# Two attentions in one kernel: maxima in the last projection product, the start, and one copy

## The chip, the cores and the metric

The kernel runs on one core of a Trainium2 chip. The metric is the device time of one execution in microseconds (us); the time of a kernel is the median of its runs.

## The reference

Two attention layers of the same shape (2,048 positions, 576 features, 32 heads of 18) stand side by side in the output. Layer A is local and dilated: a query sees eight keys, two positions apart. Layer B is a full softmax attention.

```python
qkv = (x @ wqkv).reshape(B, S, 3, H, Dh)            # S = 2048, D = 576, H = 32, Dh = 18
# A: keys at pos - 2*j, j = 0..7
logits = jnp.einsum("bhsd,bhswd->bhsw", q, kg) * scale ; mask
o = jnp.einsum("bhsw,bhswd->bhsd", softmax(logits), vg)
# B:
scores = jnp.einsum("bhqd,bhkd->bhqk", q, k) * scale
o = jnp.einsum("bhqk,bhkd->bhqd", softmax(scores), v)
# both: o.reshape(B, S, D) @ wo, and concatenate([a, b], axis=-1)
```

Everything is in single precision. The kernel keeps it with products of operands that are split into a high and a low part.

## The kernel before, in words

The order of the instructions on each engine is written by hand: what the program emits first stands first. Work for later is put in an agenda by step (`later`, `plan`), and `slot` and `due` emit what is due.

The stages, by the clock of the profiled execution:

1. *0 to 44 us.* Inputs are loaded and split, first products of layer B (L595). Ahead of them stand warm products of zeros (L561), whose results nobody reads, and the load of the exponential's table on ACT with its first use (L404).
2. *44 to 81 us.* The values of layer B (L317).
3. *81 to 402 us.* The other projections, of both layers. `stream` takes the products four at a time, in pairs of halves of the rows, and sets maxima in between (`most(j)` says how many pairs of maxima are given by the end of product j). A projection product of A leaves through `leave_a`, by a copy on ACT (L747) into `ohi`, and goes to DRAM.
4. *402 to about 1,448 us.* The attention steps of B: 512 steps, which are 32 blocks (eight groups of four heads, four blocks of 512 queries) of 16 key tiles. A step has four scores on PE (L285), four exponentials on ACT (L293), and the four weighings by the values into `po` (L800). In between PE makes maxima of later blocks (L161), VectorE reduces them (L169), and POOL computes the local attention A.
5. *To the end.* The output sums: beside the steps (`beside`, L1246), in pieces between them (L1278), and at the end. Each finished row block `y` is added on VectorE (L1285) and stored by SP (`out<-y`, L1315).

The softmax of B subtracts a row maximum ahead of the exponential. It enters the scores as two more rows of the operand `qs` (high and low part, `mh` and `mt`). A block needs 32 pairs of maxima, 1,024 pairs in all: of a pair, one matmul (L161) uses each half of the array's rows, and one reduction belongs to each. After a block's last reduction come `least` (L179), in the next step the transpose (L186), then the split on POOL (L104, L105), and then eight small DMAs on SP (`place`, L200) into `qs`. A block's first scores wait for these eight. Steps make one and a half pairs each (one whole pair, one in halves of 256 columns), and use up two; so the lead with which blocks are finished shrinks towards the end. `EARLY_PAIRS` pairs are made ahead of the first step.

There are seven PSUM banks in rotation: four for scores, three ("else") for maxima and products in the attention stage. SP is one queue, and issues in order: `qs<-mh` and `qs<-mt` are L200, `y<-wob` loads output weights (L954), `do<-n` stores a block's attention result (L835), `ks<-do` and `qs<-do` load such results back (L1171).

The lines that set the counts of maxima before:

```python
few = 7 * (NT - 4) // 4
folded_ = [args[0] == "folded" for args, _, _ in work_list]
plain = [sum(not f for f in folded_[NT - 4 : j + 1]) for j in range(len(work_list))]
most = [few + 2 * sum(folded_[:j + 1]) + (EARLY_PAIRS - few - 2 * sum(folded_)) * p // plain[-1]
        for j, p in enumerate(plain)]
```

Of the kernel before, what the change touches and what calls it, by code (L numbers as in the profile page):

```python
# [7 lines left out]
F32 = mybir.dt.float32  # L8
F32R = mybir.dt.float32r
BF16 = mybir.dt.bfloat16  # L10
AF = mybir.ActivationFunctionType
# [12 lines left out]
NT = S // 128  # L24
NB = S // 512
# [10 lines left out]
PIECES = 2 * 4 * NB  # L36


EARLY = 2
EARLY_PAIRS = EARLY * NB * PIECES + 2  # L40
AHEAD = 7

AT = [10, 67] + [13 + 55 * j for j in range(2, S // AB)]
# [18 lines left out]
def two_attentions(ctx: ExitStack, tc, xa, wa, woa, xb, wb, wob, out):  # L62
# [5 lines left out]
    nc = tc.nc  # L68
# [13 lines left out]
    def bank(kind=None):  # L82
        r = rings[kind or ring]
        r.append(r.pop(0))
        return p_bank.tile([128, 512], F32, name=f"bank{r[-1]}")
# [13 lines left out]
    ones = const.tile([2, 128], F32, name="ones")  # L99
    nc.gpsimd.memset(ones, 1.0)  # L100
    warm = const.tile([2, 8], F32, name="warm")
# [249 lines left out]
    def stream(products, most, last):  # L351

        where, ends = {}, {}  # L360
        for j in range(len(products)):
            first = j - j % 4
            turn = [((0, 0), (1, 1)), ((0, 2), (1, 3)), ((0, 1), (1, 0)), ((0, 3), (1, 2))][j % 4]
            both = []
            for r, k in turn:
                args, view, _ = products[first + k]
                if j % 4 < 2:
                    where[k] = view(bank("scores"))
                else:
                    assert sum(given) - ends[k] > 3  # L370
                parts = folded(r, *args[1:]) if args[0] == "folded" else halves(r, *args)
                both.append([(where[k], *ab, j % 4 < 2 and i == 0, j % 4 > 1 and i == len(parts) - 1)
                             for i, ab in enumerate(parts)])
            n = most(j) - given[0]
            others = last if j == len(products) - 1 else ([], [])
            n += 2 if others[0] else 0
            total = n + len(both[0])
            for r in range(2):
                for i in range(n):
                    both[r].insert((4 * i + 1 + 2 * r) * total // (4 * n), None)  # L380
            for pair in zip(*both):
                for r, p in enumerate(pair):
                    if p is None:
                        (others[r].pop(0) if others[r] else maximum(r))()
                    else:
                        ps, a, b, start, stop = p
                        nc.tensor.matmul(ps, a, b, start=start, stop=stop)  # L387
            for k in sorted(k for _, k in turn):
                if j % 4 < 2:
                    ends[k] = sum(given)  # L390
                else:
                    products[first + k][2](where[k])
            slot()
            for _ in range(min(len(posts), 2)):
                posts.popleft()()
        do_all(posts)
# [4 lines left out]

    every = slice(0, 512)

    nc.scalar.activation(warm, ones[:, :8], AF.Exp)  # L404

    with (tc.tile_pool(name="x", bufs=1, side="right") as xp,
          tc.tile_pool(name="a0", bufs=1, side="right") as a0):
        raw_room = ExitStack()
        rp = raw_room.enter_context(tc.tile_pool(name="rows", bufs=1, side="right"))
# [29 lines left out]
        def weights(pool, src, cols, engine, wide=384, spare=False):  # L439

            whole = [[], [], None, None]
            n = sum(m for _, m in cols)

            def into(c, t):
                if c < 4:
                    hi, lo = (pool.tile([128, wide], F32R, name=nm, bufs=4) for nm in ("whi", "wlo"))
                    whole[0].append(hi)
                    whole[1].append(lo)
                else:
                    hi, lo = (pool.tile([128, wide], F32R, name=nm, bufs=1) for nm in ("whh", "wll"))  # L450
                    whole[2:] = hi, lo
                split(engine, hi[:, :n], lo[:, :n], t)

            apart = cols[1][0] - cols[0][0] if len(cols) > 1 else n
            return whole, *staged(src, cols, [(apart, len(cols)), (1, cols[0][1])], into, spare)
# [59 lines left out]
        def folds(c):  # L515
            return c == 13
# [13 lines left out]
        if True:  # L530
# [3 lines left out]
            def turn_cols(i):  # L534
                return [(third * i, third), (D + third * i, third)]
# [19 lines left out]
                        at += n  # L555


            zeros = rp.tile([128, 512], F32, name="raw", bufs=5)
            nc.vector.memset(zeros, 0.0)
            for _ in range(2):  # L560
                nc.tensor.matmul(bank(), zeros[:, :128], zeros, start=True, stop=True)  # L561
            w0, w_get, w_put = weights(proj[0], wb, turn_cols(0), nc.vector, spare=True)

            xs = [inputs(xb, b, nc.vector, spare=b != 2) for b in range(NB)]
            for c in range(5):
                one, other = (load, nc.scalar.dma_start) if c % 2 == 0 else (nc.scalar.dma_start, load)
                w_get(c, one)
                xs[0][1](c, other if c < 4 else load)
            for b in range(1, NB):
                for c in range(5):  # L570
                    xs[b][1](c)
# [76 lines left out]
            for t in range(NT):  # L648
                ps = bank()
# [87 lines left out]
            def leave_a(c, b, n, ps):  # L737
                o = xp.tile([128, 512], F32, name="ohi", bufs=4)
                at = slice(0, n)
                if folds(c):  # L740
                    at, other = (slice(64 * r, 64 * r + 64) for r in (b % 2, 1 - b % 2))
                    rest = ws[c][0][2].bitcast(F32)
                    nc.scalar.activation(rest[at], ps[other], AF.Copy)
                    nc.scalar.activation(o[at], ps[at], AF.Copy)
                    nc.gpsimd.tensor_add(o[at], o[at], rest[at])
                else:
                    nc.scalar.activation(o[at], ps[at], AF.Copy)  # L747
                load(da[128 * c : 128 * c + n, HALO + 512 * b : HALO + 512 * b + 512], o[at])


            order = [t for i in (0, 8) for j in range(4) for t in (i + j, i + j + 4)]
            for t in order[:4]:
                ps = bank()
# [5 lines left out]
            work_list = []  # L759
# [10 lines left out]
            order = [(c, b) for b0 in range(0, NB, 2) for c in range(2) for b in (b0, b0 + 1)]  # L770
            order += [(c, b) for c in sorted(range(2, 14), key=a_place) for b in range(NB)]
            for c, b in order:
                n = min(128, 3 * D - 128 * c)
                work_list.append((("folded", ws[c][0], xas[b][0]) if folds(c) else
                                  (b % 2, ws[c][0], xas[b][0], slice(0, n), every),
                                  lambda ps: ps, lambda ps, c=c, b=b, n=n: leave_a(c, b, n, ps)))
            es = [None] * 4
            few = 7 * (NT - 4) // 4
            folded_ = [args[0] == "folded" for args, _, _ in work_list]
            plain = [sum(not f for f in folded_[NT - 4 : j + 1]) for j in range(len(work_list))]  # L780
            most = [few + 2 * sum(folded_[:j + 1]) + (EARLY_PAIRS - few - 2 * sum(folded_)) * p // plain[-1]
                    for j, p in enumerate(plain)]
            stream(work_list, lambda j: 7 * (j + 1) // 4 if j < NT - 4 else most[j],
                   [[lambda r=r: es.__setitem__(r, score(0, 0, 0, r, "else")), lambda r=r: maximum(r)(),
                     lambda r=r: es.__setitem__(r + 2, score(0, 0, 0, r + 2, "else"))] for r in range(2)])
# [623 lines left out]
    while step < ALL:  # L1409
        n, kt = divmod(step, NT)  # L1410
        g, b = divmod(n, NB)
# [23 lines left out]
        ps = bank() if inside and whole else None  # L1435
# [67 lines left out]
```

## Time and profile before

| | |
|---|---|
| median of 3 runs | 1578.12 us (1577.4 to 1578.15) |
| profiled execution | 1577.92 us, span 1576.1 us |
| granted TensorE clock | 1.00 in all windows |
| PE busy | 1566.0 us (99%) |
| DVE busy | 1375.7 us (87%) |
| ACT busy | 1210.7 us (77%) |
| POOL busy | 975.9 us (62%) |

The span is the time from the first to the last instruction on the chip; 1.8 us of the measured time lie outside it. PEld is the load of weights into the array, which can lie beside a product. A bracket behind a row of the timeline says how long its engine had stood idle before it and what ended that ("issue" where the profile shows no releaser). A timeline row with xN holds N instructions of one form, and its duration runs from the first to the last of them.

### The profile page before, as it was taken

The page shows a single profiled execution, that of the slowest core. Times are in us where ns is not written, and L with a number is a line of the kernel's source. Part 1 is how long each engine was busy: PE and PEld are TensorE (multiplying, and loading weights), DVE is VectorE, ACT ScalarE, POOL GpSimd, SP SyncE. Part 2 cuts the span into 40 slices and gives each one's busy share as a digit, 9 for nine tenths or more (in the row PEclk, how much of TensorE's full clock was granted, in tenths as well). Part 3 has the DMA queues.
Part 4 walks back from the last instruction along what each step waited for, and adds up shares of the span by engine and source line. Part 5 has one row for each costly group of instructions (what it writes and reads, how often), then busy time and mean ns, then how long its engine had stood idle before and what let it go on. Part 6 is the DMA issues. An engine that isn't in the chain of part 4 may idle for free.

```text
span 1576.1 us, 34876 instructions
## 1 busy us (share of the span) xinstructions
PE 1566.0 (99%) x13236; PEld 967.7 (61%) x13236; DVE 1375.7 (87%) x2333; ACT 1210.7 (77%) x2415; POOL 975.9 (62%) x807
## 2 busy tenths in 40 slices
PE   9999999999999999999999999999999999999998
PEld 7999999999544445445445445445444444545686
DVE  5189999999999999999999999999999999998633
ACT  6324432122799999999999999999999999998554
POOL 2316752212256995995896896897797798782000
PEclk9999999999999999999999999999999999999999
DMA  8848954532312362254325324422721331154311
GB/s 259 230 142 217 268 167 125 145 107 74 68 50 57 81 140 83 55 126 101 74 82 130 86 90 112 117 79 53 150 81 50 91 101 53 50 164 136 138 57 69
DMA packets 188168, 175.65 MB, mean 111 GB/s; under 512 B 119432, under 2 KB 133512, under 8 KB 186272
## 3 DMA queue, kind: packets, MB, share of 16 engines
q1 hardware_dynamic: 182992, 161.73, 37.5%
q0 software_dynamic: 4032, 10.63, 3.3%
q8 instruction: 104, 1.70, 0.5%
q10 hardware_dynamic: 976, 1.07, 0.2%
q14 instruction: 64, 0.52, 0.1%
HBM read 98.77 MB, written 73.47 MB: 109 GB/s over the span
## 4 chain that ended last, share of the span: by engine, by line
PE 95%; DVE 3%; DMA 1%; ACT 0%; POOL 0%; issue 0%; SPq 0%; DVEq 0%; POOLq 0%; ACTq 0%
PE po L800 30%; PE bank L285 19%; PE bank L161 18%; PE bank L387 16%; PE bank L1381 4%; PE bank L1278 3%; DVE mx L169 2%; PE bank L595 2%; PE bank L317 2%; DMA dqk<-olo 1%; PE bank L1246 0%; DMA first<-xb 0%; ACT e L293 0%; PE bank L1210 0%; POOL olo L549 0%
## 5 line engine op out<-in xcount | busy, mean ns | idle before, releaser
L169 DVE TENSOR_REDUCE mx<-bank 128x2 f32<-128x512 f32 x2048 | 1276.8, 683 | 109.5 <-PE bank L161 82.2
L293 ACT ACTIVATE e<-bank 128x512 f32<-128x512 f32 x2048 | 1047.7, 604 | 81.5 <-PE bank L285 77.1
L161 PE MATMUL bank<-ks,qs 54*128 54x512 f32 (+1 forms) x2464 | 784.6, 380 | 2.4 <-DVE mx L169 0.5
L161 PEld LDWEIGHTS bank<-ks,qs 54*128 54x128 f32 x2464 | 402.8, 184 | 388.7 <-DVE mx L169 343.4
L285 PE MATMUL bank<-qs,ks 56*128 56x512 f32 x2048 | 591.6, 425 | 0.0
L800 PE MATMUL po<-e,v 128*19 128x512 f32 x4096 | 531.8, 598 | 0.4
L285 PEld LDWEIGHTS bank<-qs,ks 56*128 56x128 f32 x2048 | 308.6, 184 | 20.4 <-ACT e L293 14.5
L1021 POOL TENSOR_TENSOR pr<-aq,akv 128x1024 f32<-128x1024 f32 x72 | 158.5, 2203 | 15.5 <-DMA akv<-da 12.7
L1063 POOL TENSOR_TENSOR pr<-lg,akv 128x1024 f32<-128x1024 f32 x72 | 158.3, 2199 | 0.6
L800 PEld LDWEIGHTS po<-e,v 128*19 128x19 f32 x4096 | 73.5, 97 | 138.5 <-issue 133.2
L1025 POOL TENSOR_TENSOR pr<-pr 128x1024 f32<-128x1024 f32 x64 | 152.7, 2385 | 5.0
L747 ACT ACTIVATE ohi<-bank 128x512 f32<-128x512 f32 x52 | 28.2, 595 | 139.1 <-issue 111.7
L387 PE MATMUL bank<-xhi,ahi 64*128 64x512 f32 x448 | 113.2, 386 | 0.0
L387 PE MATMUL bank<-xlo,ahi 64*128 64x512 f32 x448 | 107.6, 387 | 0.0
L1381 PE MATMUL bank<-wohi,at 64*128 64x288 f32 x480 | 103.3, 304 | 0.0
L387 PE MATMUL bank<-xhi,alo 64*128 64x512 f32 x416 | 103.0, 387 | 0.0
L1064 POOL TENSOR_TENSOR pr<-pr 128x512 f32<-128x512 f32 x72 | 92.5, 1285 | 5.6
L1381 PEld LDWEIGHTS bank<-wohi,at 64*128 64x128 f32 x480 | 74.6, 184 | 27.5 <-ACT e L293 23.8
L549 POOL TENSOR_TENSOR olo<-olo,ohi 128x512 fp32r<-128x512 f32 x36 | 46.2, 1293 | 68.3 <-ACT ohi L548 60.7
L437 POOL TENSOR_TENSOR alo<-raw,ahi 128x512 fp32r<-128x512 f32 x13 | 16.9, 1296 | 113.6 <-ACT ahi L436 79.7
L104 POOL CAST mh<-mt 128x32 fp32r<-128x32 f32 x32 | 6.8, 212 | 110.6 <-DVE mt L186 85.5
L1381 PE MATMUL bank<-wolo,at 64*128 64x288 f32 x240 | 70.2, 293 | 0.0
(215 smaller groups left out, 1856.2 us busy)
## 6 DMA issues: line engine op xcount, KB each, us to landing
do<-n SPq DMA_DIRECT2D x30, 512.0 KB
da<-ohi SPq DMA_DIRECT2D x52, 256.0 KB
akv<-da SPq DMA_DIRECT2D x64, 175.5 KB
out<-y SPq DMA_DIRECT2D x31, 288.0 KB
qs<-dqk SPq DMA_DIRECT2D x30, 288.0 KB
ks<-dqk SPq DMA_DIRECT2D x30, 288.0 KB
at<-dao SPq DMA_DIRECT2D x60, 128.0 KB
rec<-drec SPq DMA_DIRECT2D x29, 256.0 KB
```

The lines of the kernel that those rows point to most:

```text
L161: return awaiting(nc.tensor.matmul(ps if part is None else ps[:, 256 * r : 256 * r + 256], qs[at, b, p, 128 * t : 128 * t + 128], ks[at, p ...
L169: nc.vector.tensor_reduce(at, ps.rearrange("q (s n) -> q s n", s=2), axis=AX.X, op=ALU.max)
L285: awaiting(nc.tensor.matmul(ps, ks[at, p, 128 * kt : 128 * kt + 128], qs[at, b, p], start=True, stop=True))
L293: nc.scalar.activation(e, ps, AF.Exp, scale=SCALE)
L387: nc.tensor.matmul(ps, a, b, start=start, stop=stop)
L800: nc.tensor.matmul(po[32 * i : 32 * i + 19], vs[g][:, kt, 19 * i : 19 * i + 19], es[i], start=kt == 0, stop=kt == NT - 1)
L1021: nc.gpsimd.tensor_mul(pr, ap(st["q"][:, 2 * c], (SUB, 2), (0, W), (1, SUB)), window(st["k"], c))
L1025: nc.gpsimd.tensor_add(st["pr"], st["pr"], pr)
L1063: nc.gpsimd.tensor_mul(at, ap(st["lg"], (0, 2), (SUB, W), (1, SUB)), window(st["v"], c))
L1064: nc.gpsimd.tensor_add(at[:, :, :4], at[:, :, :4], at[:, :, 4:])
L1278: nc.tensor.matmul(sums_[r], *both[r][i], start=i == 0, stop=last)
L1381: return nc.tensor.matmul(ps, a, b, start=r == k == 0, stop=r == 1 and k == len(both[1]) - 1)
```

## The change

Four edits. `EARLY_PAIRS` is 256 instead of 258, and the counts are by rule: two pairs in a folded product, three in another, and what is left, two, in the last. The first use of the exponential's table stands behind ACT's four first DMA issues. Nine warm products of 128 columns take the place of two of 512. The last product of A's projection is copied out of its bank by VectorE.

```diff
-EARLY_PAIRS = EARLY * NB * PIECES + 2
+EARLY_PAIRS = EARLY * NB * PIECES
...
-    nc.scalar.activation(warm, ones[:, :8], AF.Exp)
...
-            zeros = rp.tile([128, 512], F32, name="raw", bufs=5)
+            zeros = rp.tile([128, 512], F32, name="raw", bufs=5)[:, :128]
             nc.vector.memset(zeros, 0.0)
-            for _ in range(2):
-                nc.tensor.matmul(bank(), zeros[:, :128], zeros, start=True, stop=True)
+            for _ in range(9):
+                nc.tensor.matmul(bank()[:, :128], zeros, zeros, start=True, stop=True)
...
                 xs[0][1](c, other if c < 4 else load)
+            nc.scalar.activation(warm, ones[:, :8], AF.Exp)
...
+                elif (c, b) == order[-1]:
+                    nc.vector.tensor_copy(o[at], ps[at])
                 else:
                     nc.scalar.activation(o[at], ps[at], AF.Copy)
...
-            folded_ = [args[0] == "folded" for args, _, _ in work_list]
-            plain = [sum(not f for f in folded_[NT - 4 : j + 1]) for j in range(len(work_list))]
-            most = [few + 2 * sum(folded_[:j + 1]) + (EARLY_PAIRS - few - 2 * sum(folded_)) * p // plain[-1]
-                    for j, p in enumerate(plain)]
+            narrow = [args[0] == "folded" for args, _, _ in work_list]
+            each_takes = [0] * (NT - 4) + [2 if f else 3 for f in narrow[NT - 4 :]]
+            most = [few + sum(each_takes[: j + 1]) for j in range(len(work_list))]
+            assert 0 <= most[-1] - EARLY_PAIRS < 2
+            most[-1] = EARLY_PAIRS
```

Where the order moves, shown at three places. VectorE at the end of the last projection product, before; `mx<-bank` are the reductions, `m_83` the maxima of the block that is just complete:

```order
L169 TENSOR_REDUCE mx<-bank_5945 128x2
L169 TENSOR_REDUCE mx<-bank_5952 128x2
L169 TENSOR_REDUCE mx<-bank_5969 128x2
L169 TENSOR_REDUCE mx<-bank_5974 128x2
L169 TENSOR_REDUCE mx<-bank_5979 128x2
L179 TENSOR_REDUCE m_83<-mx 128x16
L169 TENSOR_REDUCE mx<-bank_5988 128x2
L169 TENSOR_REDUCE mx<-bank_5991 128x2
L169 TENSOR_REDUCE mx<-bank_5998 128x2
L186 STREAM_TRANSPOSE mt<-m_83 128x32
L169 TENSOR_REDUCE mx<-bank_6022 128x2
```

and after, from the same place:

```order
L169 TENSOR_REDUCE mx<-bank_5963 128x2
L169 TENSOR_REDUCE mx<-bank_5970 128x2
L169 TENSOR_REDUCE mx<-bank_5989 128x2
L169 TENSOR_REDUCE mx<-bank_5996 128x2
L746 COPY ohi<-bank_5850 128x512
L169 TENSOR_REDUCE mx<-bank_6021 128x2
L179 TENSOR_REDUCE m_83<-mx 128x16
L169 TENSOR_REDUCE mx<-bank_6014 128x2
L169 TENSOR_REDUCE mx<-bank_6039 128x2
```

Eight reductions belonged to the last product (to `bank_5998`) and four do now; the copy stands behind them, and the block's `least` comes in the first step instead of inside the product.

SP where block 29's maxima go out, before:

```order
L1171 DMA ks_89<-do 126x1x512 x4
L200 DMA qs_1511<-mh 2x8x32 x4
L200 DMA qs_1511<-mt 2x8x32 x4
L954 DMA y<-wob 126x576
L835 DMA do<-n 128x2x512
L845 DMA drec<-den 128x16
```

and after:

```order
L1173 DMA ks_89<-do 126x1x512 x4
L956 DMA y<-wob 126x576
L837 DMA do<-n 128x2x512
L200 DMA qs_1525<-mh 2x8x32 x4
L200 DMA qs_1525<-mt 2x8x32 x4
L847 DMA drec<-den 128x16
```

The eight L200 have moved behind one load of weights and one store of a result.

SP where the last block's maxima (block 31's) go out, before:

```order
L1190 DMA aq<-do 18x2x512 x6
L1315 DMA out<-y 128x576 x3
L200 DMA qs_1511<-mh 2x8x32 x4
L200 DMA qs_1511<-mt 2x8x32 x4
L1315 DMA out<-y 128x576 x2
L868 DMA do<-n 128x2x512
```

and after:

```order
L1192 DMA aq<-do 18x2x512 x6
L1317 DMA out<-y 128x576 x4
L200 DMA qs_1525<-mh 2x8x32 x4
L200 DMA qs_1525<-mt 2x8x32 x4
L1317 DMA out<-y 128x576
L870 DMA do<-n 128x2x512
```

One more store of output rows stands ahead of the eight. Lines of the attention stage are two higher after the change (L800 is L802, L1315 is L1317); L161, L169, L200 and L285 are the same.

## The prediction

> **What bounds the kernel now.** I began with the page's head, its busy times and its chain, to see which engine sets the end:
>
> ```profile
> span 1576.1 us, 34876 instructions
> PE 95%; DVE 3%; DMA 1%; ACT 0%; POOL 0%; issue 0%; SPq 0%; DVEq 0%; POOLq 0%; ACTq 0%
> L169 DVE TENSOR_REDUCE mx<-bank 128x2 f32<-128x512 f32 x2048 | 1276.8, 683 | 109.5 <-PE bank L161 82.2
> ```
>
> TensorE carries 95% of the chain; the reductions of the maxima are VectorE's largest group, and each waits for a matmul of line 161. But a share of the whole hides stages with different limits. The window of the last 128 us (duration, then busy time of PE, PEld, DVE, ACT, POOL, granted clock, DMA share, GB/s):
>
> ```profile
> 1448.00:1576.00 128.00, 123.76 (x1366) 90.24 (x1362) 64.05 (x132) 71.72 (x143) 6.79 (x14) 1.00 0.26 94
> ```
>
> Here only PE is nearly full, VectorE and ACT only to about half: whatever PE waits for in this part is paid at once. The change touches four places: the start, the hand-over from projections to attention near 402 to 412, and, because the maxima move, two late places where a block's row maxima must have landed before PE may score with them. I take them in the order of time. Two runs of the kernel that are within 0.2% (3.16 us of 1578.12, so 1574.97 to 1581.28) I call the same, about what a measurement of this kernel can tell.
>
> **The start: warm products and the table.** The timeline of the first microseconds (start, duration, what, idle before):
>
> ```profile
> 0.74 1.28 ACT L404 ACT_TABLE_LOAD   x1 [0.74 <-PEq L1495]
> 0.92 0.48 DVE L559 MEMSET raw<- 128x512 f32 x1 [0.92 <-PEq L1495]
> 0.97 0.38 ACTq L430 DMA_DIRECT2D first<-xb  x1
> 1.46 0.50 PEld L561 LDWEIGHTS bank<-raw 128*128 128x128 f32 x2 [1.46 <-DVE raw L559]
> 1.46 3.78 PE L561 MATMUL bank<-raw 128*128 128x512 f32 x4 [1.46 <-DVE raw L559]
> 3.33 0.33 PEld L561 LDWEIGHTS bank<-raw 128*128 128x128 f32 x1 [0.52 <-issue]
> 5.17 0.43 DVE L104 CAST xhi<-first 128x512 fp32r<-128x512 f32 x1 [3.77 <-DMA first<-xb]
> 5.75 0.94 PE L595 MATMUL bank<-xhi,whi 128*128 128x512 f32 x3 [0.51 <-DVE xhi L104]
> ```
>
> The first product at 5.75 waits for a cast, and the cast for the first piece of x, whose load ACT issues at 0.97, behind 0.23 us that the table load already held it. With the table load behind ACT's four issues, that load can go at 0.74, so 0.2 us earlier at most; I take half, −0.1. The table load itself (1.28) then stands ahead of the first split on ACT, which has to wait for a load of the same group (the cast at 5.17 shows when such a load is in), so it is covered; without that cover it would cost its 1.28. The warm products go from two of 512 columns to nine of 128: 1,152 moving columns instead of 1,024, so by columns 3.78 × 1,152/1,024 = 4.25 us, begun about 0.35 earlier because the memset has a quarter of the width: over by 5.4, under the 5.75 of the first product. But 18 passes now need 18 weight loads instead of 4. At 0.33 each and nothing overlapped, 18 × 0.33 = 5.9 us from 1.1 is 7.0, 1.3 too late. The rows show loads beside running products (two loads end at 1.96 while the first product runs), so I take the columns. Start: −0.1, range −0.2 to +1.3, the upper end as a rival below. The Trainium skill ("TensorE: Matmul & The Clock Gate", Part 1) says that PE's queue can pull weight loads ahead of running matmuls; the loads at 1.46 agree for two of them, and no row here shows eighteen short ones in a line; by that rule the start stays at −0.1.
>
> **The hand-over.** "Three pairs per product, two in the last" changes less than its words: worked through with the kernel's counts, every unfolded product took three pairs already and every folded one two, only the last took four. So only the last product changes: two pairs of maxima fewer, four reductions, and all later maxima stand two pairs further on. VectorE, ACT and the chain around it:
>
> ```profile
> 391.62 10.85 DVE L169 TENSOR_REDUCE mx<-bank 128x2 f32<-128x512 f32 x17 [0.21 <-PE bank L161]
> 403.06 0.69 DVE L169 TENSOR_REDUCE mx<-bank 128x2 f32<-128x512 f32 x1 [0.59 <-PE bank L161]
> 404.06 0.69 DVE L169 TENSOR_REDUCE mx<-bank 128x2 f32<-128x512 f32 x1 [0.30 <-PE bank L161]
> 407.50 1.09 ACT L747 ACTIVATE ohi<-bank 128x512 f32<-128x512 f32 x2 [1.87 <-issue]
> 408.66 0.62 PE bank L161 x2
> 409.76 0.98 PE po L800 x8
> L815 DVE COPY o<-po x10: 671/681/681, 441.6 to 1413.9; 128x512 f32<-128x512 f32 x10
> ```
>
> A reduction costs 10.85/17 = 0.64 in line, so four are 2.55 of VectorE's time in a stretch in which PE waits for VectorE's banks. That is the most that can go. Against it stands the copy of the last product, now on VectorE: 0.68 by the copy of the same size, where ACT took 1.09/2 = 0.55 and has then less ahead of its exponentials. 2.55 − 0.68 = 1.87. The gaps of 0.59 and 0.30 ahead of single reductions show that VectorE in turn waits for PE here, so not all comes back: −1.7. If PE alone sets the pace, the four matmuls are the gain, 4 × 0.23 = 0.9 (half a pair's time in the chain, 0.62 for two being the widest row); if the copy is wholly covered, 2.6. Range −0.9 to −2.6.
>
> **Block 29's maxima.** A block's maxima leave VectorE, are split on POOL, and reach the score's operand through eight small DMAs on SP (L200). SP issues in order. Two pairs later puts the eight of block 29 behind `y<-wob` and `do<-n`, which stood behind them. Before:
>
> ```profile
> 1400.85 2.33 SPq L200 DMA_DIRECT2D qs<-mh  x4
> 1403.29 3.00 SPq L200 DMA_DIRECT2D qs<-mt  x4
> 1406.33 0.44 SPq L954 DMA_DIRECT2D y<-wob  x1
> 1406.83 0.39 SPq L835 DMA_DIRECT2D do<-n  x1
> 1407.42 0.35 PE L161 MATMUL bank<-ks,qs 54*128 54x256 f32 x1 [0.33 <-issue]
> SPq L200 <- POOL mt L105: 4.9, 1, 4.9
> SPq L200 <- DMA ks<-do: 0.9, 1, 0.9
> 1399.00:1403.00 4.00, 4.00 (x34) 1.67 (x34) 3.87 (x8) 4.00 (x9) 3.92 (x5) 1.00 0.46 175
> 1403.00:1407.00 4.00, 4.00 (x34) 1.68 (x32) 3.69 (x7) 4.00 (x10) 3.70 (x5) 1.00 0.21 74
> y<-wob SPq DMA_DIRECT2D x3, 283.5 KB
> do<-n SPq DMA_DIRECT2D x1, 512.0 KB
> ```
>
> The last of the eight leaves SP at 1406.29 and PE goes 1.13 later, having stood still for 0.33: this wait is already the last one, with no slack. The line on `ks<-do` shows that an L200 issue also waits for a DMA that was issued eight places ahead. After the change the seventh and eighth have `y<-wob` and `do<-n` at that place, so they can't be issued until these have landed. When is that? The rings are at 0.46 of 16 engines, some seven, with 175 GB/s, which is the queue left by `ks<-do`; at that share the 0.21 × 4 us after 1403 end by 1404.8. On those seven, `y<-wob` takes 283.5 KB/175 = 1.7 us, and 7/16 of `do<-n` 229 KB/175 = 1.3: 1407.8. Add 0.6 until this is signalled (half of the 1.13, my choice), 0.55 for the last issue and the 1.13: 1410.1, against 1407.42, is +2.7. If both big ones ran through the seven alone, 795.5 KB/175 = 4.7, it would be the upper end, +4.7 (rounded). If SP can send them into its 4.9 us of waiting for POOL and they land early, only part of their issue times 0.44 + 0.39 is left: +0.3. Who waits behind it: PE, in order, with all scores and maxima behind.
>
> The Trainium skill ("DMA: Bandwidth & Descriptors", Queues, rings and completion order) says that each DMA engine consumes descriptors in ring order; if so, small L200 pieces cannot overtake `do<-n`. The trace agrees so far: these pieces of 2 KB issued from 1400.85 were not all in until 1407.4. Without that rule the term would be nearer to +0.8 and the sum 1.9 lower.
>
> **Two more pairs at the end.** Near 1478 the pairs run out; after the change one more pair is taken inside a `beside` quarter of the output sums and one is spread as halves over two steps. Starts of successive weighings:
>
> ```profile
> 1473.95 1.05 PE L800 MATMUL po<-e,v 128*19 128x512 f32 x8
> 1478.15 1.05 PE L800 MATMUL po<-e,v 128*19 128x512 f32 x8
> 1482.73 1.05 PE L800 MATMUL po<-e,v 128*19 128x512 f32 x8
> 1486.75 1.05 PE L800 MATMUL po<-e,v 128*19 128x512 f32 x8
> 1491.87 1.05 PE L800 MATMUL po<-e,v 128*19 128x512 f32 x8
> ```
>
> A segment with a pair beside it takes 4.20, those without 4.58, 4.02, 5.12. One of kind 4.20 replaces the 4.02, and 0.2 for halves beside the next: +0.4, ends +0.2 (the difference alone) and +1.0 (four matmuls of 0.23 in full).
>
> **Block 31's maxima.** Its eight L200 are now behind a fourth store `out<-y`, which was behind them:
>
> ```profile
> 1494.94 2.33 SPq L200 DMA_DIRECT2D qs<-mh  x4
> 1497.38 2.19 SPq L200 DMA_DIRECT2D qs<-mt  x4
> 1502.95 10.44 SPq L1315 DMA_DIRECT2D out<-y  x2
> 1502.47 0.46 DVE L1285 TENSOR_TENSOR y<-bank,y 128x288 f32<-128x288 f32 x1 [0.56 <-PE bank L1278]
> 1507.36 0.63 PE L285 MATMUL bank<-qs,ks 56*128 56x512 f32 x4
> ```
>
> The fourth store is the first of the row at 1502.95: it waits for VectorE's sum of 1502.47. The scores of block 31 begin at 1507.36 (1,984 scores, 496 steps, lie ahead). Issues of L200 take 1494.94 to 1499.57, 4.63, and the 1.13 until PE may go, 5.76. Begun at 1502.95 + 0.35, they release PE at 1509.1: +1.7. If the signal needs half the 1.13, +1.2; if the store's own pieces, issued just ahead, delay them as the rows near 1407 show in small, +2.5. There is no cover: PE sets the end here.
>
> **Sum against the profiled execution** (1577.92, its span and 1.8 around it): −0.1 − 1.7 + 2.7 + 0.4 + 1.7 = +3.0, so 1580.9; the median of before stands 0.2 above its profiled execution, so **1581.1**. Its own range goes from 1578.7 (block 29 at +0.3) to 1583.1 (block 29 at +4.7).
>
> **The rivals.**
> - *Both transfers hidden, not slower (0.17).* The two big DMAs go into SP's idle 4.9 us, and the store finds its sum earlier. For it: that idle time, and all later times move by −1.8 alike. Against: the 0.33 us at 1407, no slack. It holds if block 29's maxima land before 1407.1 and block 31's before 1507.4 on the clock of before. 1577.92 − 0.1 − 1.7 + 0.4 + 0.2 = 1576.7; with the hand-over at −2.6, 1575.8, near the bound of faster.
> - *A long wait at block 29 (0.12).* `do<-n` drains through the seven engines alone: 1581.1 + 2.0 = 1583.1. For it: the low 175 GB/s. Against: with the other nine engines free, only 7/16 of `do<-n` should have to queue there.
> - *VectorE becomes the bound at the hand-over (0.08).* The copy waits for PE's last matmul with the next reductions queued behind it, and PE waits for their banks: the gain of 1.7 turns into +0.7, 1581.1 + 2.4 = 1583.5. For it: VectorE is busy 10.85 us in one piece just ahead. Against: its gaps after 403.
> - *Nine weight-bound warm products (0.06).* The first product moves to 7.0: 1581.1 + 1.4 = 1582.5.
>
> **How the numbers follow.** The forecast has 0.57. About 0.25 of that and 0.23 of the slower rivals' 0.26 lie above 1581.28: slower 0.48. From the hidden case 0.04 and from the forecast's lower tail 0.03 is below 1574.97 (a gain at the hand-over above my bound): faster 0.07. Same: 0.45. The range leaves a tenth on either side: from the hidden case's 1576.5 to 1583.9, above the long wait's 1583.1.
>
> **What would show it.** In the profile after: the first product (L595's) start within 0.3 of 5.6; weighing begins (`po`) near 408; a gap on PE at block 29 of about 3 us with the eight L200 issues ending near 1408 to 1409; a second gap of 1.7 ahead of block 31's first scores. I am wrong if either gap is missing, if the warm products run past 5.7, or if `po` begins no earlier than 409.

## The result, and the profile after

The changed kernel takes 1586.33 us (median of 6 runs, 1584.29 to 1587.96), the kernel before 1578.13 in the same comparison: 1.0052 of it, 95% interval 1.0039 to 1.0064. It is slower by 8 us, outside the predicted range of 1576.5 to 1583.9. The profiled execution took 1586.90. From the page of the changed kernel, its head and its chain:

```profile
span 1585.1 us, 34916 instructions
PE 80%; DMA 3%; DVE 3%; POOL 3%; ACT 1%; SPq 1%; issue 0%; DVEq 0%; ACTq 0%; POOLq 0%
```

PE's share of the chain fell from 95% to 80%: the chain back from the end now leaves PE at the late waits. The table compares the two traces instruction by instruction: the same instruction, counted from the front of its line, starts so much later (or earlier, with a minus) than before:

| place, time of before | later by, us | that stage adds | predicted |
|---|---|---|---|
| first product, 5.75 | 0.11 | | |
| last of the first products, 43.73 | 1.84 | 1.84 | -0.1 |
| projections, 370.4 | 1.34 | -0.50 | 0 |
| first weighing, 409.69 | -0.54 | -1.88 | -1.7 |
| step 460, 1406.03 | -0.88 | -0.34 | 0 |
| step 463, 1412.52 (block 29) | 4.75 | 5.63 | +2.7 |
| step 488, 1478.15 | 4.78 | 0.03 | 0 |
| step 495, 1504.43 (two pairs) | 5.29 | 0.51 | +0.4 |
| step 497, 1512.85 (block 31) | 9.00 | 3.71 | +1.7 |
| end | 9.02 | 0.02 | 0 |

Every place of a loss was foreseen; three sizes were not. (The projections' -0.50 comes with a shorter wait of PE for a split on ACT near 190 us, 0.64 instead of 1.31.) The rows of the changed kernel's timeline and windows at block 29 (the windows: duration, busy time of PE, PEld, DVE, ACT, POOL, then granted clock, DMA share, GB/s):

```profile
1395.86 0.77 SPq L956 DMA_DIRECT2D y<-wob  x1
1399.78 0.40 SPq L837 DMA_DIRECT2D do<-n  x1
1400.28 2.80 SPq L200 DMA_DIRECT2D qs<-mh  x4
1404.09 3.87 SPq L200 DMA_DIRECT2D qs<-mt  x4
1405.15 1.05 PE L802 MATMUL po<-e,v 128*19 128x512 f32 x8
1409.34 0.55 PE L161 MATMUL bank<-ks,qs 54*128 54x256 f32 x1 [3.14 <-DMA drec<-den]
1417.27 1.05 PE L802 MATMUL po<-e,v 128*19 128x512 f32 x8
1407.00:1411.00 4.00, 1.66 (x8) 1.38 (x8) 0.64 (x2) 0.83 (x2) 3.92 (x3) 0.75 0.34 84
1411.00:1415.00 4.00, 4.00 (x22) 1.67 (x24) 2.23 (x5) 2.43 (x6) 2.17 (x3) 0.50 0.99 321
1415.00:1419.00 4.00, 4.00 (x30) 1.28 (x22) 3.01 (x6) 3.08 (x7) 0.99 (x1) 0.90 0.48 176
```

`y<-wob` and `do<-n` stand ahead of the eight, and the last of them leaves SP at 1407.96. As forecast, the seventh and the eighth issue wait for these two to land, 0.5 us each in SP's own waits. Three issues ahead of them wait 2.2 in all for `ks<-do`, where before the eighth alone waited 0.9. PE stands for 3.14 us instead of 0.33. (The page names `drec<-den` as releaser, since it landed last; what PE needs are the eight.) That is 2.8 more, as predicted. But then the granted clock reads 0.50: from 0.75, 0.50 and 0.90 of three windows of 4 us it was low for 2.0 + 4.0 + 0.8 = 6.8 us, and in it PE did half its work. From 1405.15 to 1417.27, three steps take 12.12 us, where the same three took 6.49 before (1406.03 to 1412.52 in the table): 5.63 lost, half to the longer wait and half to the clock.

Block 31:

```profile
1487.10 21.48 SPq L1317 DMA_DIRECT2D out<-y  x4
1508.67 2.35 SPq L200 DMA_DIRECT2D qs<-mh  x4
1511.13 2.48 SPq L200 DMA_DIRECT2D qs<-mt  x4
1514.94 1.22 PE L285 MATMUL bank<-qs,ks 56*128 56x512 f32 x4 [2.14 <-issue]
1518.83 0.63 PE L285 MATMUL bank<-qs,ks 56*128 56x512 f32 x4
1512.00:1516.00 4.00, 1.86 (x20) 1.52 (x18) 0.46 (x1) 0.20 (x1) 0.00 (x0) 0.85 0.02 4
1516.00:1520.00 4.00, 4.00 (x46) 3.93 (x44) 1.44 (x4) 2.61 (x6) 0.00 (x0) 0.72 0.02 4
```

The eight go out behind the fourth store, PE stands for 2.14, and again the clock falls: four scores in 1.22 us, later four in 0.63. Low for 1.2 + 2.2 = 3.4 us.

The start:

```profile
0.74 0.43 ACTq L428 DMA_DIRECT2D first<-xb  x1
1.06 4.21 PE L559 MATMUL bank<-raw 128*128 128x128 f32 x18 [1.06 <-DVE raw L557]
5.28 0.52 ACT L434 ACTIVATE whi<-first 128x384 fp32r<-128x384 f32 x1 [1.08 <-DMA first<-wb]
5.86 1.65 PE L594 MATMUL bank<-xhi,whi 128*128 128x512 f32 x3 [0.59 <-ACT whi L434]
9.72 0.85 PE L594 MATMUL bank<-xhi,whi 128*128 128x512 f32 x3
```

The warm products end at 5.27, where the columns put them (4.21 us). x comes earlier, but w's first chunk later, and its split (5.28, it was 4.54) now holds the first product. Then three products take 1.65 us, where three take 0.85 from 9.72 on: half rate, which the profile before does not show (0.94 at 5.75).

### The profile page after: what moved, and what is told of

Same layout as the page of the kernel before. It is cut to its first block, busy times and chain, and to the rows that moved or that the text cites. A ratio compares the mean times of both kernels' runs of the same rounds, so it can differ in the third digit from the quotient of the medians.

```text
span 1585.1 us, 34916 instructions
## 1 busy us (share of the span) xinstructions
PE 1571.2 (99%) x13252; PEld 978.2 (62%) x13252; DVE 1376.9 (87%) x2335; ACT 1209.6 (76%) x2413; POOL 974.7 (61%) x807
## 4 chain that ended last, share of the span: by engine, by line
PE 80%; DMA 3%; DVE 3%; POOL 3%; ACT 1%; SPq 1%; issue 0%; DVEq 0%; ACTq 0%; POOLq 0%
PE po L802 28%; PE bank L285 18%; PE bank L161 16%; PE bank L387 11%; PE bank L1383 3%; PE bank L1280 3%; DVE mx L169 2%; DMA dqk<-olo 2%; POOL pr L1065 1%; DMA raw<-xa 1%; POOL pr L1066 1%; ACT e L293 0%; PE bank L1248 0%; DMA do<-n 0%; POOL pr L1067 0%
## 5 line engine op out<-in xcount | busy, mean ns | idle before, releaser
L169 DVE TENSOR_REDUCE mx<-bank 128x2 f32<-128x512 f32 x2048 | 1277.3, 683 | 114.4 <-PE bank L161 87.1
L161 PE MATMUL bank<-ks,qs 54*128 54x512 f32 (+1 forms) x2466 | 786.3, 380 | 4.9 <-DMA drec<-den 3.1
L161 PEld LDWEIGHTS bank<-ks,qs 54*128 54x128 f32 x2466 | 404.1, 184 | 391.0 <-DVE mx L169 341.9
L285 PE MATMUL bank<-qs,ks 56*128 56x512 f32 x2048 | 594.5, 427 | 2.3 <-issue 2.1
L802 PE MATMUL po<-e,v 128*19 128x512 f32 x4096 | 533.1, 600 | 0.4
L285 PEld LDWEIGHTS bank<-qs,ks 56*128 56x128 f32 x2048 | 309.9, 185 | 22.7 <-ACT e L293 13.5
L802 PEld LDWEIGHTS po<-e,v 128*19 128x19 f32 x4096 | 73.6, 97 | 138.8 <-issue 133.5
L387 PE MATMUL bank<-xlo,ahi 64*128 64x512 f32 x448 | 112.1, 387 | 0.0
```

The costliest lines, as they stand in the source:

```text
L161: return awaiting(nc.tensor.matmul(ps if part is None else ps[:, 256 * r : 256 * r + 256], qs[at, b, p, 128 * t : 128 * t + 128], ks[at, p ...
L169: nc.vector.tensor_reduce(at, ps.rearrange("q (s n) -> q s n", s=2), axis=AX.X, op=ALU.max)
L285: awaiting(nc.tensor.matmul(ps, ks[at, p, 128 * kt : 128 * kt + 128], qs[at, b, p], start=True, stop=True))
L802: nc.tensor.matmul(po[32 * i : 32 * i + 19], vs[g][:, kt, 19 * i : 19 * i + 19], es[i], start=kt == 0, stop=kt == NT - 1)
```

## The experiments

**The maxima alone, and everything but the maxima.** Two theories: (1) late small DMAs make PE wait, and the clock's fall behind each wait costs about as much again; (2) the other edits make the loss. The first kernel is the one before with these lines of the change only:

```diff
-EARLY_PAIRS = EARLY * NB * PIECES + 2
+EARLY_PAIRS = EARLY * NB * PIECES
... (and `most` by `each_takes`, as in the change)
```

> The kernel before with the counts of maxima of the change and nothing else. Theory 1 (the eight small DMAs of blocks 29 and 31 stand behind other transfers, PE waits, and the granted clock falls to 0.50 for some us after each wait): hand-over -1.9, block 29 +5.6, two more pairs +0.5, block 31 +3.7, drift of the attention stage -0.3, so about 1578.1 + 7.6 = 1585.7, with PE gaps near 1406 and 1513 and granted clock 0.50 behind both. Rival (the other three edits, above all the short warm products and the copy on VectorE, make the loss): within 2 us of 1578.1.

1583.63 us, 1.0041 (1.0024 to 1.0058): 5.6 of the 8 us, 2 less than I expected. In the profile the hand-over gives -1.91, block 29 costs 4.96, the two pairs 0.47, block 31 3.80. The profiled execution took 1591.06, because in the projections PE waited 3.5 us for a split on ACT, where it had waited 1.3 in the profile before:

```profile
192.12 0.50 PE L387 MATMUL bank<-xhi,whi 64*128 64x512 f32 x1 [3.51 <-ACT olo L547]
192.00:196.00 4.00, 3.88 (x22) 3.03 (x24) 2.08 (x3) 1.43 (x4) 2.93 (x3) 0.60 1.03 368
```

The clock fell there too. The second kernel is the changed one with the old counts (258 and the old `most`):

> The changed kernel with the counts of maxima of the kernel before: nine short warm products, table behind the first DMA issues, last copy on VectorE. Theory 1: no gap at blocks 29 and 31, and only the start's loss is left, 1578.1 + 1.3 = 1579.4, with first products at half rate until near 9.5 us. Rival (these three edits make the loss): near 1586.

1579.64 us, 1.0013 (1.0003 to 1.0023). Blocks 29 and 31 cost 0.62 and 0.00. At the hand-over it is 0.58 later than before: with all four pairs still there, the copy costs VectorE about its 0.68. (Its profiled execution took 1582.54: at 83.45 PE had stood for 1.54 us, for ACT, and the granted clock read 0.50 for 3.41 us behind that.) So the maxima make most of the loss, theory 1.

**The order on SP.** One number moves the eight DMAs of each block of the last group one step forward, ahead of the transfers they had fallen behind (both lines go on as in the kernel):

```diff
-            later(2 if g == NG - 1 else 5, lambda: posts ...
+            later(1 if g == NG - 1 else 5, lambda: posts ...
```

> The changed kernel, but the last group's eight small DMAs are emitted one step after the split instead of two, which puts them ahead of the weights' load and the result's store at block 29 and ahead of the fourth output store at block 31 again. Theory 1: both waits and both stretches of half clock go, 1586.3 - 5.6 - 3.7 = 1577.0. Rival (the two pairs more, late, cost whatever the order on SP, because a block's maxima are finished too late by themselves): no better than 1584.

1578.30 us, 0.9998 (0.9988 to 1.0007): 8 us of the changed kernel's time are back, and the rival falls. But the 1.3 expected beyond that are missing. The same comparison of this profile with the one before shows where: it is 1.64 ahead at step 460 and 0.51 behind at step 463.

```profile
1399.20 2.33 SPq L200 DMA_DIRECT2D qs<-mh  x4
1401.90 4.90 SPq L200 DMA_DIRECT2D qs<-mt  x4
1407.92 0.35 PE L161 MATMUL bank<-ks,qs 54*128 54x256 f32 x1 [2.48 <-DMA qs<-mt]
1403.00:1405.00 2.00, 2.00 (x20) 0.86 (x16) 1.84 (x4) 2.00 (x5) 1.78 (x4) 1.00 0.08 28
1405.00:1407.00 2.00, 0.45 (x7) 0.00 (x0) 0.88 (x2) 0.94 (x2) 1.92 (x2) 1.00 0.03 10
1407.00:1409.00 2.00, 1.07 (x12) 0.79 (x16) 0.45 (x1) 0.54 (x2) 1.28 (x1) 1.00 0.50 109
```

The eight start 1.65 earlier than before (1400.85), but the second four take 4.90 instead of 3.00: each waits for one of the four loads `ks<-do` ahead. These loads still move 28 GB/s, at a share of 0.08, from 1403 to 1405. Some seven rings had moved 175 GB/s, 25 each, so this is the rest of about one ring. PE, which comes earlier by the hand-over's gain, stands until that rest is in. How long the rest lasts differs between executions: with the same order on SP the block cost 2.14 here, and 3.54 and 0.89 in two later profiles, while a profile of a kernel with the old counts (nine short warm products, below) brought a lead of 0.84 past the same loads as 0.74.

**Is it the clock?** The changed kernel with matmuls into a bank that is written anew afterwards, ahead of both waits (`keep_warm(n, k)` gives k of them):

```diff
+        if kt == NT - 2 and n + 1 == 29:
+            keep_warm(n, 16)
+        if kt == 0 and n == 31:
+            keep_warm(n - 1, 12)
```

> The changed kernel with 16 matmuls ahead of the wait at block 29 and 12 ahead of the wait at block 31, into a bank that is written anew afterwards: results that nobody reads, about 3.4 and 2.6 us of work in the gaps. Theory 1 with the clock as a part of its own: the waits stay but the granted clock stays at 1.00, so -2.8 and -1.5, 1586.3 - 4.3 + up to 0.7 for matmuls that outlast the gaps = 1582.0 to 1582.7. Rival (the steps behind the wait are slow because ACT and VectorE have run dry, not because of the clock): 1586.3 or above.

1583.04 us, 1.0032 (1.0020 to 1.0045), 3.3 below the changed kernel, from which it differs only in that the gaps are filled.

```profile
1403.89 3.96 PE L1414 MATMUL bank<-qs,ks 54*128 54x512 f32 x16
1405.00:1407.00 2.00, 2.00 (x10) 1.60 (x9) 0.00 (x0) 0.00 (x0) 2.00 (x2) 1.00 0.03 4
1407.00:1409.00 2.00, 1.94 (x16) 1.14 (x18) 0.44 (x1) 0.55 (x2) 1.89 (x2) 1.00 0.71 208
```

ACT and VectorE stand idle (0.00 busy from 1405 to 1407), and yet the granted clock is 1.00 and the steps behind run at their usual 2.0 us. Block 29 costs 3.61 instead of 5.63, block 31 2.74 instead of 3.71. The order's experiment agrees: behind its gap of 2.48 us, at a clock of 1.00, the block cost 2.14, which is the longer wait and no more. The engines that run dry are not what makes the steps slow; the clock is.

**Each block by itself.** Block 29 put ahead and block 31 left late, and the reverse (the same line, with 1 for one block and 2 for the others):

> The changed kernel with block 29's small DMAs put ahead again, and block 31's left behind the fourth output store. Theory 1: block 31's price alone, a wait of 2.1 and 1.6 for the clock that falls behind it, 1578.3 + 3.7 = 1582.0. Rival without a fall of the clock in most executions: 1580.4.

> The changed kernel with block 31's small DMAs put ahead again, and block 29's left behind the weights' load and the result's store. Theory 1: block 29's price alone, 5.6 in the changed kernel's profile against 2.1 that the order before shows too, 1578.3 + 3.5 = 1581.8, with the granted clock at 0.50 behind the wait. Rival (the wait alone, without the clock): 1579.0.

Block 31 late: 1579.79 us, 1.0013 (1.0004 to 1.0022), 2.2 below what I expected and near the rival's 1580.4. In the profile block 31 cost 1.96, about its wait of 1.72, and block 29, put ahead, still 3.54 by the backlog that the order's experiment showed:

```profile
1406.76 0.35 PE L161 MATMUL bank<-ks,qs 54*128 54x256 f32 x1 [2.35 <-DMA qs<-mt]
1407.00:1411.00 4.00, 4.00 (x24) 1.96 (x22) 2.23 (x4) 2.62 (x6) 2.30 (x3) 0.61 0.99 270
1510.68 0.73 PE L285 MATMUL bank<-qs,ks 56*128 56x512 f32 x4 [1.72 <-DMA qs<-mt]
1508.00:1512.00 4.00, 2.28 (x32) 2.05 (x30) 0.61 (x3) 0.76 (x2) 0.00 (x0) 1.00 0.02 4
```

The clock stayed up behind 1.72 us and fell behind 2.35 (0.61 in the window). Block 29 late: 1582.44 us, 1.0024 (1.0012 to 1.0036), against 1581.8 expected; block 29 cost 6.00 with the clock at 0.50. Over the order's experiment the two cost 1.5 and 4.1 apart and 8.0 together. A wait has its price; the fall of the clock comes on top in some executions only.

**The copy.** As the order's experiment, with the last copy on ACT again:

> The changed kernel with the last group's small DMAs one step earlier, and with the last product's copy on ACT again. Theory 1 (VectorE sets the pace of the hand-over, and its copy of 0.68 costs what the prediction charged): weighing begins 0.3 to 0.7 earlier against the last projection product than with the copy on VectorE. Rival (the two copies stand ahead of ACT's exponentials in the chain): 0.5 to 0.6 later. In the median within 0.7 of 1578.3 either way.

1578.30 us, 0.9998 (0.9989 to 1.0007). The hand-over gains 1.88 here, and 1.87 with VectorE's copy: neither theory. With four reductions fewer, the copy is off the path on either engine.

**The start.** The kernel before with nine short warm products, and the kernel before with the table's first use moved:

> The kernel before with nine warm products of 128 columns in place of two of 512. Theory 1 (the first products at half rate until 9.5 us in the changed kernel's profile were the clock's free-running phase, and the shape matters little): first products in the profile at a spacing of 0.23 from the start on, the first stage ends within 0.3 of 43.7, 1578.1 to 1578.5. Rival (short products do not bring the clock up in time): half rate until 9 us, the first stage 1.5 to 2 us later, 1579.7.

> The kernel before with the exponential's first use behind ACT's four DMA issues. Theory 1 (the other order of issues of the two queues brings w's first chunk later, at 5.28 instead of 4.54, and the first product waits for its split on ACT instead of x's on VectorE): first product 0.1 to 0.2 later, at 5.85 to 5.95, 1578.2. Rival (prediction: x comes earlier): first product 0.1 to 0.2 earlier, 1578.0.

1578.33 us, 1.0005 (0.9991 to 1.0019), and 1579.01 us, 1.0004 (0.9995 to 1.0014): neither can be told from no change by its time. With the table's use moved the first product comes 0.29 later, in theory 1's direction but beyond its 0.2. The first products in their profiles:

```profile
5.62 1.22 PE L595 MATMUL bank<-xhi,whi 128*128 128x512 f32 x3 [0.35 <-DVE xhi L104]
6.04 1.65 PE L594 MATMUL bank<-xhi,whi 128*128 128x512 f32 x3 [0.79 <-ACT whi L434]
```

The upper row, nine short products, changes to full rate at once and ends the first stage 0.31 later; the lower one, with two long ones, runs at half rate and ends it 2.10 later. So the half rate does not need short products. Of the nine profiles with the table's use moved, four show it (the changed kernel, this one, the copy on ACT, block 29 late) and end the first stage 1.8 to 2.2 later; five run at full rate from about 5.9 and lose 0.2. Of the five without the move none loses more than 0.73.

What parts the four from the five can be read from the clock's records, which change in steps of 3.413 us (last section). Counted back in such steps from the falls late in the same execution, a step ends at 6.12, 6.46, 6.56 and 6.81 in the four slow starts, with 0.59 to 0.79 us of standing between the warm products and the first real one in it; full rate comes with the end of the next step, at 9.53, 9.87, 9.98 and 10.22, to within one product. In four of the five others a step ends while the warm products still run, in the fifth with 0.57 us of standing in it. The gap is 0.59 to 1.19 us with the table's use moved and 0.34 to 0.51 without, so a longer gap would make the slow start more frequent. That is a reading of 14 profiles; no run set where the steps fall, and the timed runs are compatible with both.

**Where the hand-over's gain went, and a faster kernel.** If a backlog swallows it, moving the backlog should free it. The old results `ks<-do` are loaded in two lots, planned at steps 6 and 24 of the last group. As the order's experiment, and (a part of one line):

```diff
-... (6, lambda: fetch_old(1, 0, 2)), (24, lambda: fetch_old(1, 2, 4)) ...
+... (15, lambda: fetch_old(1, 0, 2)), (24, lambda: fetch_old(1, 2, 4)) ...
```

> The changed kernel with the last group's small DMAs one step earlier, and with the four loads ks<-do that stand directly ahead of block 29's small DMAs planned nine steps later, so that they go behind them. Theory 1 (block 29 waits for a backlog of transfers on SP's rings, and without it the gain of the hand-over reaches the end): no PE wait near 1406, 1578.1 - 1.6 at the hand-over and through the steps + 0.5 for the two late pairs - 0.3 for the wait that the kernel before already has = 1576.7. Rival (POOL, which splits the maxima at about 1399 whatever comes before, or another engine sets block 29's time): the wait stays at 2 us or more, 1578.3 as with the order alone.

1578.37 us, 0.9999 (0.9991 to 1.0008). Block 29's wait is gone (-0.37 there). But:

```profile
1412.47 3.61 SPq L1173 DMA_DIRECT2D ks<-do  x4
1418.01 0.61 SPq L845 DMA_DIRECT2D den<-o  x1
1427.75 0.25 DVE L846 RECIPROCAL den<-den 128x16 f32<-128x16 f32 x1 [2.54 <-DMA den<-o]
1429.20 0.38 PE L161 MATMUL bank<-ks,qs 54*128 54x256 f32 x1 [2.39 <-DVE mx L169]
```

The small load `den<-o` now stands behind the four, a reciprocal on VectorE waits for it with all reductions behind, and PE waits for VectorE: 2.4 are lost by step 471, which neither theory had. Next, the lots at steps 24 and 31, with the start of the kernel before:

> The change's maxima and its copy on VectorE, the start of the kernel before, the last group's small DMAs one step earlier, and the old results ks<-do fetched in two lots at steps 24 and 31 of the last group instead of 6 and 24, so that the first lot stands ahead of block 30's small DMAs, where the second stood, and nothing of it ahead of block 29's. Theory 1 (the hand-over's gain was lost to block 29's backlog, and in the run before to a reciprocal of VectorE that waited for a small load behind the moved backlog): no PE wait at blocks 29, 30 or 31 and none on VectorE near 1428, so 1578.3 - 1.6 + 0.5 - 0.3 = 1576.9. Rival (another wait takes its place again): 1578 or more.

1580.47 us, 1.0012 (1.0004 to 1.0021), as the rival had it. There is no wait at 1406 or 1428, and the profile is 2.88 ahead at step 485; then PE waits for `ao<-do` behind the second lot, and the clock falls:

```profile
1468.17 1.04 PE L1249 MATMUL bank<-qs,ao 54*128 54x288 f32 x4 [1.79 <-DMA ao<-do]
1470.00:1473.00 3.00, 3.00 (x18) 1.59 (x12) 1.20 (x3) 1.03 (x3) 0.00 (x0) 0.50 0.45 152
```

From step 485 to step 488 5.1 are lost, for a wait of 1.79. The last run has the lots at 24 and 40, the second behind those loads.

> As the run before that moved the old results to steps 24 and 31, but its second lot at step 40, behind the loads ao<-do that PE waited for at 1468 and behind the other old results. Theory 1 (every wait so far came from one more load standing ahead of a small one on SP's seven busy rings): PE stands at none of 1406, 1428 and 1468, the lead of 2.9 of that run's profile at step 474 is kept but for the 0.5 of the two late pairs, and the median is 1576.0 to 1577.0 against 1577.8 to 1578.3 for before. Rival (a wait turns up at the next place again, at the fourth lot or at block 31): 1578 or more.

1575.34 us, 0.9985 (0.9976 to 0.9994): below both kernels, and 0.7 below the range that I expected. Windows of its profile over the three places:

```profile
1400.00:1416.00 16.00, 15.97 (x126) 6.71 (x126) 14.66 (x25) 15.94 (x32) 11.09 (x10) 1.00 0.65 190
1460.00:1476.00 16.00, 16.00 (x168) 10.27 (x165) 15.25 (x28) 10.59 (x20) 2.26 (x4) 1.00 0.53 189
1500.00:1516.00 16.00, 16.00 (x202) 12.41 (x200) 7.12 (x18) 8.12 (x16) 2.20 (x4) 1.00 0.18 71
```

PE is full in all three, at a clock of 1.00. The lead of 2.95 at step 488 reaches the end as 2.42, less by the 0.53 of the two pairs. The run also has the start of the kernel before; the two runs on the start stood 0.0 and 0.7 above that kernel, so this is the smaller part of the 3.0 between this run and the order's experiment.

## Why the prediction was wrong, point by point

- *The start* (-0.1, measured +1.84 in this profile). The step that failed is that x's load sets the first product: ACT's split of w does, 0.11 later in all. Its rival, weight loads that bind, was wrong as well; the columns were right. The rest is half-rate products, which come and go between executions.
- *The edit of the maxima* changes the last product only, and the hand-over gains 1.88 (1.7 predicted). That the number fits is partly luck: the working let the four reductions give 2.55 and charged the copy with 0.68, but fewer maxima alone gain 1.91 and the copy's engine makes no difference, so two errors cancel.
- *Block 29* (+2.7, measured 5.63). The wait was sized rightly, 3.14 instead of 0.33 us, and in the main for the right reason. The step that failed is "whatever PE waits for in this part is paid at once" as the whole price. PE's own clock falls behind the wait, for 6.8 us, worth 2.8. The working had no term for that.
- *Two more pairs* (+0.4): measured 0.51, and 0.46 to 0.55 in the nine other profiles that have them.
- *Block 31* (+1.7): a wait of 2.14, inside its range, and 3.4 us at half clock behind it, 3.71 together. The same step failed.
- *The drift* of -0.34 in the attention stage and the -0.50 of the projections were not in the sum.
- *The rivals.* "Both transfers hidden" failed: the small DMAs were late by the transfers named. The long wait at block 29 did not come: 3.14 us is the wait of the forecast. VectorE did not become the bound, and the warm products were not bound by their weights. No rival held a second cost behind a wait, so the range ended 2.4 below the median.

Shown by experiment: that the maxima make most of the loss, that the order on SP is what matters in them, that filling the gap keeps the clock, and that the loads `ks<-do` ahead of small DMAs held back the hand-over's gain. Read from profiles alone: where the clock's steps fall. Open: why one ring of `ks<-do` takes longer in one execution than in another.

## What to carry to other kernels

Price a new wait of the engine that bounds the kernel at its length and once more: where it may lower that engine's clock, the steps behind it pay too. A gain early in a kernel reaches the end only if no later wait takes it; look for the row where that engine already waits a little, here 0.33 us. When a small transfer is late, list what stands ahead of it in its queue, and then what would stand behind it if that moved: here the wait moved twice before it went.

## What the hardware showed

- An idle gap much shorter than 3 us can halve the granted clock. It fell behind gaps of PE of 3.88, 3.51, 3.50, 3.14, 2.35, 2.14 (twice), 1.79 and 1.54 us, and did not behind 2.48 (the order's experiment), 2.39 and 2.35 (the first run with the loads moved) and 1.72. So the length alone does not decide. It stayed low for 3.41 or 6.83 us.
- In one execution the clock falls at whole multiples of 3.413 us: the 105.81 us between the two falls of the changed kernel (1409.00 and 1514.81) are 31 of them, the 1221.97 us from 192.83 to 1414.80 in the kernel with the maxima alone are 358, and the other seven distances fit as well. Counted in these steps, PE had stood for 1.54 to 3.41 us of each step that ended with a fall, and, behind the start, for at most 1.70 us of any that did not: the gap of 2.48 is cut by a step's end into 1.57 and 0.91, the 2.35 without a fall into 1.70 and 0.65, and the 2.35 with a fall lies in one step but for 0.03. In these 14 profiles about half a step of idleness is the limit, and whether a gap of some 2 us reaches it is a matter of where it falls.
- The Trainium skill ("TensorE: Matmul & The Clock Gate", Part 1) names at least one idle window of about 3.4 us, free-running, as the condition. The steps, and low stretches of one and two of them, agree with such a window; but 1.54 to 1.79 us of idleness are no whole window, so here the measurement decides.
- The granted clock of the windows does not show the slow start: in the changed kernel it reads 1.00 from 6 to 9 us, where three products take 1.65 instead of 0.85 us. There, the rows' own durations decide.
- Small DMAs on a queue keep to its order: the trace of each late block agrees with what the Trainium skill ("DMA: Bandwidth & Descriptors", Queues, rings and completion order) says of descriptors consumed in ring order. Before, the first of block 29's pieces is issued at 1400.85 and moves at 1404.19, 3.3 us later, behind `ks<-do`; in the last run, with no large load ahead, it moves 1.24 us after its issue (1398.23 and 1399.47). With the change's counts PE stood 1.2 to 3.9 us at block 29 while these loads were ahead and the gap was not filled, and not at all in the three runs that moved them.
